# Decoding the first network's weights during the attention scores, with squares in PSUM and GpSimd clamping

## The chip, the core and the metric

The kernel runs on one core of a Trainium2 chip. The metric is the device time of one execution in microseconds (us), less is better. The engines go by the names of the profile: PE (TensorE matmul) with PEld (its weight loads), DVE (VectorE), ACT (ScalarE), POOL (GpSimd) and SP (SyncE, which here issues the DMAs). Each engine works through its own instructions in program order.

## The reference

An attention over channels is followed by two feed-forward networks, over 6016 tokens of 256 channels:

```python
qn = q / (np.linalg.norm(q, axis=1, keepdims=True) + 1e-06)
kn = k / (np.linalg.norm(k, axis=1, keepdims=True) + 1e-06)
s = kn.transpose(0, 2, 1) @ qn / tau            # 256 x 256
a = np.exp(s - s.max(-1, keepdims=True)); a /= a.sum(-1, keepdims=True) + 1e-09
x = v @ a                                       # 6016 x 256
h = x @ w_in1;  x = (h * np.cos(h)) @ w_out1    # 256 -> 2048 -> 256
h = x @ w_in2;  x = (h / (1 + np.exp(-h))) @ w_out2
```

q, k, v are float32, the four weight matrices float64 (4.19 MB each).

## The kernel before

It has three stages that bear on the change.

**Scores.** q and k lie together in 47 chunks of 128 rows, taken in 25 groups (`GROUPS`: two of one chunk, 22 of two, one of one). For each group g SP loads `qk` (eight buffers), PE multiplies into the scores S (`emit_scores`, L261), ACT squares into an SBUF tile `sq` with three buffers (L284), DVE adds to `acc` (L289). The scores of the last two groups (`LATE`) are emitted behind the norm matmuls N (L296, L300). Then come square roots, reciprocals, E (L320 to L325), the transposes to ET, eight warm-up matmuls among them.

**Weights.** A float64 matrix is loaded as 64-bit integers in pieces of 512 elements per partition and turned into float32 by `Weights.decode`: ACT takes the absolute value of the upper words (L136), GpSimd scales the lower words (L137), DVE clamps (L140), shifts (L141) and puts the sign in (L144), GpSimd adds the rounded low part (L147). For w_out1 GpSimd also makes a high and a low part (L150, L151): float32 products are done in three passes over high and low parts. Of the eight pieces of w_in1 two are loaded and decoded within the scores (`W1_LOADS`, `W1_DECODES`), the others between scores and fold; `to=w1` is a float32 tile.

**Fold and units.** The attention matrix is folded into w_in1: `emit_w(j)` multiplies ET by a quarter of w1 (pw, L356), ACT writes the high part of `wa[j]` (L362), DVE the low part (L364). Then 96 units follow (12 token blocks b of 512 or 496 tokens, eight units m each). A unit has `emit_h` (PE, twelve matmuls h, L395), `emit_first` (ACT L407, DVE L408), `emit_cos` (ACT L415, DVE L416), and, one unit later, `emit_split` (ACT L423 high, DVE L424 low) and, two units later, `emit_o1` (PE, twelve matmuls, L434). Units 2j and 2j + 1 of a block need `wa[j]` for h and `wo1[j]` for o1. The high and low parts of v for a block come from `load_v` and `split_v`. In block 0 each unit also loads and decodes a piece of w_out1; `emit_w(0)` to `emit_w(2)` stand ahead of unit 0, `emit_w(3)` ahead of unit 1, as does `load_v(1)`. From block 1 on the second network's weights are decoded in the same way, and the second network follows; that code is not touched.

PSUM has a pool `ps_o` (S, N, pw of j = 2 and 3, o1) and a pool `ps_h` (h, the transposes, pw of j = 0 and 1), two buffers each, allotted in turn.

Of the kernel before, what the change touches and what calls it, by code (L numbers as in the profile page):

```python
# [66 lines left out]
def attention_then_two_ffns(ctx: ExitStack, tc: tile.TileContext, qk, vT, tau, w_in1, w_out1, w_in2, w_out2, outT):  # L67
# [34 lines left out]
    class Weights:  # L102

        def __init__(self, name, srcs, parts=None, to=None, forms=None, pool=io, bufs=2):
            self.name, self.srcs, self.parts, self.to, self.pool, self.bufs = name, srcs, parts, to, pool, bufs
            self.forms = forms
            self.raws, self.loaded, self.decoded = {}, 0, 0

        def load(self, k=1):
            for i in range(self.loaded, min(self.loaded + k, len(self.srcs))):
                raw = self.pool.tile([P, PIECE], I64, tag="raw", name=f"raw_{self.name}{i}", bufs=self.bufs)
# [3 lines left out]
                self.loaded = i + 1  # L117

        def decode(self):
# [5 lines left out]
            a = self.srcs[i].shape[1]  # L125
            if self.to is None:
                t = io.tile([P, NS * P], F32, tag="wv", name=f"wv_{self.name}{i}")
                v = t[:, :PIECE].rearrange("p (a b) -> p a b", a=a)
            else:
                v = self.to[i]  # L130
            vi = v.bitcast(I32)

            def word(t, d):
                return raw.bitcast(d).rearrange("p (a b t) -> p a b t", a=a, t=2)[:, :, :, t]

            nc.scalar.activation(v, word(1, F32), AF.Abs)  # L136
# [4 lines left out]
            nc.vector.tensor_scalar(  # L141
                out=vi, in0=vi, scalar1=3, scalar2=0x3FFFFFFF, op0=ALU.logical_shift_left, op1=ALU.bitwise_and
            )
            nc.vector.scalar_tensor_tensor(  # L144
                out=vi, in0=word(1, I32), scalar=-0x40000000, in1=vi, op0=ALU.bitwise_and, op1=ALU.bitwise_or
            )
            nc.gpsimd.tensor_tensor(out=vi, in0=vi, in1=word(0, I32), op=ALU.add)  # L147
            if self.parts is not None:
                hi, lo = self.parts[i]
                nc.gpsimd.tensor_scalar(out=hi, in0=v, scalar1=1.0, scalar2=1.0, op0=ALU.mult, op1=ALU.mult)  # L150
                nc.gpsimd.tensor_tensor(out=lo, in0=v, in1=hi.bitcast(F32), op=ALU.subtract)  # L151
            if self.forms is not None:
                self.forms(i, t.rearrange("p (s b) -> p s b", b=P))

# [10 lines left out]

    def w_in(w, name, parts=None, to=None, **kw):
        n = PIECE // CH
        src = w.rearrange("(a p) f -> p a f", p=P)
        cut = [slice(j * n, (j + 1) * n) for j in range(NPIECE)]
        return Weights(  # L170
            name,
            [src[:, :, c] for c in cut],
            parts and [[t[:, :, c] for t in parts] for c in cut],
            None if to is None else [to[:, :, c] for c in cut],
            **kw,
        )

    def w_out(w, name, **kw):
        n = PIECE // C
# [639 lines left out]
```

## Time and profile before

| | |
|---|---|
| median of 3 runs | 1044.47 us (1042.96 to 1044.87) |
| the profiled execution | 1042.51 us, its span 1040.7 us |
| PE busy | 1010.5 us, 97% |
| DVE busy | 927.2 us, 89% |
| ACT busy | 751.7 us, 72% |
| POOL busy | 326.1 us, 31% |
| mean granted clock of TensorE | 0.995 |
| HBM traffic | 68.75 MB read, 39.65 MB written |

The page gives one execution as the profiler recorded it. In its slices of a fortieth of the span, PE shows 8 to 9 tenths in the first five and 9 in nearly all others. Busy shares are averages over stages with different limits, so the stages have to be looked at one by one: a view of windows gives each engine's busy time in a stretch, the granted clock (1.00 is 2.4 GHz, 0.50 is 1.2 GHz) and the DMA rate; the chain of waits goes back from the last instruction to what released each; the timeline lists instructions in order, with the idle time of the engine before each and what ended it; the view of a tile lists the instructions that read or write it.

### The profile page before, as it was taken

The page shows a single profiled execution, that of the slowest core. Times are in us where ns is not written, and L with a number is a line of the kernel's source. Part 1 is how long each engine was busy: PE and PEld are TensorE (multiplying, and loading weights), DVE is VectorE, ACT ScalarE, POOL GpSimd, SP SyncE. Part 2 cuts the span into 40 slices and gives each one's busy share as a digit, 9 for nine tenths or more (in the row PEclk, how much of TensorE's full clock was granted, in tenths as well). Part 3 has the DMA queues.
Part 4 walks back from the last instruction along what each step waited for, and adds up shares of the span by engine and source line. Part 5 has one row for each costly group of instructions (what it writes and reads, how often), then busy time and mean ns, then how long its engine had stood idle before and what let it go on. Part 6 is the DMA issues. An engine that isn't in the chain of part 4 may idle for free.

```text
span 1040.7 us, 17012 instructions
## 1 busy us (share of the span) xinstructions
PE 1010.5 (97%) x6593; PEld 936.3 (90%) x6593; DVE 927.2 (89%) x1166; ACT 751.7 (72%) x1194; POOL 326.1 (31%) x301
## 2 busy tenths in 40 slices
PE   8977899999999999999999799999999999999998
PEld 7846788888998988899998799999999999999998
DVE  6989999999999899988778689999989989899997
ACT  6545567667666766666666688888887887887885
POOL 2357754646655466450100011111111111111110
PEclk9989999999999999999999999999999999999999
DMA  9822212242351532532046650220220221122001
GB/s 354 288 69 87 81 41 91 77 164 103 116 187 30 170 124 76 179 124 72 17 161 242 250 227 12 83 90 11 80 90 22 69 89 55 45 80 88 13 11 40
DMA packets 56544, 109.49 MB, mean 105 GB/s; under 512 B 2832, under 2 KB 37648, under 8 KB 56464
## 3 DMA queue, kind: packets, MB, share of 16 engines
q1 hardware_dynamic: 56320, 108.28, 30.5%
q8 instruction: 52, 0.85, 0.3%
q14 instruction: 28, 0.23, 0.1%
q10 hardware_dynamic: 144, 0.13, 0.0%
HBM read 68.75 MB, written 39.65 MB: 104 GB/s over the span
## 4 chain that ended last, share of the span: by engine, by line
PE 83%; DVE 12%; ACT 2%; DMA 1%; issue 1%; SPq 0%; DVEq 0%; ACTq 0%
PE o L499 20%; PE h L395 20%; PE o L434 20%; PE xz L499 12%; PE ys L499 9%; DVE acc L289 2%; DVE lo L424 2%; DVE t L408 2%; DVE t L416 1%; PE pw L356 1%; DMA qk<-qk_dram 1%; DVE wv_wo L144 1%; DVE wv_wo L140 1%; DVE wv_wo L141 1%; ACT t L407 0%
## 5 line engine op out<-in xcount | busy, mean ns | idle before, releaser
L458 DVE TENSOR_TENSOR lo<-t,hi 128x744 fp32r<-128x744 f32 (+3 forms) x190 | 207.5, 1095 | 34.4 <-ACT hi L455 33.1
L499 PE MATMUL o<-hi,wo 128*128 128x248 f32 (+1 forms) x1330 | 232.6, 275 | 0.0
L450 POOL TENSOR_TENSOR t<-t 128x248 f32<-128x248 f32 (+1 forms) x94 | 67.8, 721 | 456.0 <-DVE t L449 407.8
L455 ACT ACTIVATE hi<-t 128x744 fp32r<-128x744 f32 (+3 forms) x190 | 178.5, 940 | 32.5 <-PE o L499 31.6
L499 PEld LDWEIGHTS o<-hi,wo 128*128 128x128 f32 x1330 | 201.8, 192 | 0.0
L395 PE MATMUL h<-xhi,wa 128*128 128x496 f32 (+1 forms) x768 | 195.9, 378 | 3.1 <-DVE wa L364 3.1
L434 PE MATMUL o<-hi,wo 128*128 128x496 f32 (+1 forms) x768 | 193.9, 375 | 0.0
L499 PE MATMUL o<-lo,wo 128*128 128x248 f32 (+1 forms) x665 | 182.9, 275 | 0.0
L415 ACT ACTIVATE t<-t,half_pi 128x992 f32<-128x992 f32 (+1 forms) x96 | 108.7, 1133 | 81.7 <-DVE t L408 81.6
L395 PEld LDWEIGHTS h<-xhi,wa 128*128 128x128 f32 x768 | 146.1, 190 | 22.0 <-issue 4.4
L434 PEld LDWEIGHTS o<-hi,wo 128*128 128x128 f32 x768 | 145.0, 189 | 17.1
L407 ACT ACTIVATE t<-h 128x992 int32<-128x992 f32 (+1 forms) x96 | 96.5, 1005 | 80.1 <-PE h L395 71.0
L408 DVE SCALAR_TENSOR_TENSOR t<-t,h 128x992 f32<-128x992 int32 (+1 forms) x96 | 114.8, 1196 | 41.5 <-ACT t L407 41.3
L499 PE MATMUL xz<-x2hi,wi 128*128 128x248 f32 (+1 forms) x768 | 143.7, 275 | 0.0
L424 DVE TENSOR_TENSOR lo<-t,hi 128x992 fp32r<-128x992 f32 (+1 forms) x96 | 141.6, 1474 | 1.2 <-ACT hi L423 1.2
L499 PEld LDWEIGHTS o<-lo,wo 128*128 128x128 f32 x665 | 127.7, 192 | 0.0
L434 PE MATMUL o<-lo,wo 128*128 128x496 f32 (+1 forms) x384 | 114.2, 379 | 9.9 <-DVE lo L424 9.9
L416 DVE TENSOR_TENSOR t<-h,t 128x992 f32<-128x992 f32 (+1 forms) x96 | 114.9, 1197 | 5.6 <-ACT t L415 1.2
L499 PEld LDWEIGHTS xz<-x2hi,wi 128*128 128x128 f32 x768 | 116.6, 192 | 0.1
L499 PE MATMUL ys<-x2hi,wi 128*128 128x248 f32 (+1 forms) x576 | 112.2, 276 | 3.9 <-ACT u L774 3.1
L395 PE MATMUL h<-xlo,wa 128*128 128x496 f32 (+1 forms) x384 | 113.3, 377 | 0.0
L499 PE MATMUL xz<-x2lo,wi 128*128 128x248 f32 (+1 forms) x384 | 105.6, 275 | 0.0
(128 smaller groups left out, 1679.4 us busy)
## 6 DMA issues: line engine op xcount, KB each, us to landing
qk<-qk_dram SPq DMA_DIRECT2D x22, 512.0 KB, 7.3
raw_wo<-w_out_dram SPq DMA_DIRECT2D x16, 512.0 KB, 5.0
xshi<-yhi SPq DMA_DIRECT2D x8, 868.0 KB, 5.9
xslo<-ylo SPq DMA_DIRECT2D x8, 868.0 KB, 6.9
x2hi<-xshi SPq DMA_DIRECT2D x8, 868.0 KB, 5.6
x2lo<-xslo SPq DMA_DIRECT2D x8, 868.0 KB, 7.7
wo_dram<-stage_wo SPq DMA_DIRECT2D x7, 896.0 KB, 4.5
wo<-wo_dram SPq DMA_DIRECT2D x7, 896.0 KB, 7.5
```

What stands on the lines that cost most here:

```text
L289: nc.vector.tensor_tensor(out=acc[:, :n], in0=acc[:, :n], in1=sq[:, :n], op=ALU.add)
L395: nc.tensor.matmul(hp[:, s, :n], lhsT, rhs, start=(i == 0), stop=(i == len(todo) - 1))
L407: nc.scalar.activation(k, hp[:, :, :n], AF.Copy, scale=1.0 / TWO_PI, bias=0.25)
L408: nc.vector.scalar_tensor_tensor(out=t[:, :, :n], in0=k, scalar=-TWO_PI, in1=hp[:, :, :n], op0=ALU.mult, op1=ALU.add)
L415: nc.scalar.activation(t[:, :, :n], t[:, :, :n], AF.Sin, bias=half_pi)
L416: nc.vector.tensor_tensor(out=t[:, :, :n], in0=hp[:, :, :n], in1=t[:, :, :n], op=ALU.mult)
L424: nc.vector.tensor_tensor(out=lo[:, :, :n], in0=t[:, :, :n], in1=hi[:, :, :n].bitcast(F32), op=ALU.subtract)
L434: nc.tensor.matmul(o[:, e, :n], wo1_at(i, f)[:, e * P : (e + 1) * P], columns(parts[k][:, s, :n]), start=(f == 0 and (i, k) == PASSES[0]), ...
L450: eng.tensor_tensor(out=t[:, 7, :c], in0=t[:, 3, :c], in1=t[:, 6, :c], op=ALU.subtract)
L455: nc.scalar.activation(hi[:, sl, :c], t[:, 1:][:, sl, :c], AF.Copy)
L458: nc.vector.tensor_tensor(out=lo[:, sl, :c], in0=t[:, 1:][:, sl, :c], in1=hi[:, sl, :c].bitcast(F32), op=ALU.subtract)
L499: nc.tensor.matmul(out, w[:, p, ka - 1], columns(x[r][:, kb - 1, : out.shape[-1]]), start=(start and i == 0), stop=(stop and i == 2), skip ...
```

## The change

- Pieces of w_in1 and w_out1 have 1024 elements (`LARGE`), four for each matrix, from a pool of three raw buffers that both share.
- `decode` is cut into `begin` (ACT absolute value, GpSimd scaling, and the clamp, now on GpSimd), `join` (DVE shift and sign, GpSimd add) and `split` (high part by a copy on ACT, low part on GpSimd). The second network's pieces go on in the old form.
- w_in1: loads at groups 0, 6, 12, 18, `begin` at 2, 8, 14, 20, `join` at 4, 10, 16, 22, all within the scores. v's first block is loaded at group 15 and split at group 21. Nothing is decoded between scores and fold.
- Squares go to a PSUM tile of `ps_h` (two buffers) instead of SBUF (three).
- The norms of q come ahead of those of k; ten warm-up matmuls instead of eight.
- `emit_w(0)` and `emit_w(1)` stand ahead of unit 0, `emit_w(2)` at unit 1, `emit_w(3)` at unit 3. w_out1's steps follow `WO1_STEPS`, one entry for each unit of block 0, with one `begin` and `join` ahead of `emit_w(0)` and one `begin` behind `emit_w(1)`.
- `pro.close()`, the pools behind it and `load_v(1)` move from unit 1 to unit 7; the second network's first two loads both stand at unit 7.

```diff
+W1_LOADS = range(0, 24, 6)
+W1_BEGIN = range(2, 26, 6)
+W1_JOIN = range(4, 28, 6)
+V_LOAD, V_SPLIT = 15, 21
+WO1_STEPS = [("split", "join"), ("load", "begin"), ("split",), ("join", "begin"), ("split",), ("join",), ("split",), ()]
...
+        def round_low(self, raw):
+            low = self.word(raw, 0, I32)
+            nc.gpsimd.tensor_scalar(
+                out=low, in0=low.bitcast(U32), scalar1=2.0**-29, scalar2=1.0, op0=ALU.mult, op1=ALU.mult
+            )
+        def shift_and_sign(self, raw, v):
+            vi = v.bitcast(I32)
+            nc.vector.tensor_scalar(
+                out=vi, in0=vi, scalar1=3, scalar2=0x3FFFFFFF, op0=ALU.logical_shift_left, op1=ALU.bitwise_and
+            )
+            nc.vector.scalar_tensor_tensor(
+                out=vi, in0=self.word(raw, 1, I32), scalar=-0x40000000, in1=vi, op0=ALU.bitwise_and, op1=ALU.bitwise_or
+            )
+            nc.gpsimd.tensor_tensor(out=vi, in0=vi, in1=self.word(raw, 0, I32), op=ALU.add)
...
+        def begin(self):
...
+            nc.scalar.activation(v, self.word(raw, 1, F32), AF.Abs)
+            self.round_low(raw)
+            nc.gpsimd.tensor_scalar(out=v, in0=v, scalar1=WORD_MIN, scalar2=WORD_MAX, op0=ALU.max, op1=ALU.min)
+            self.begun.append((i, raw, v))
+        def join(self):
+            i, raw, v = self.begun.pop(0)
+            self.shift_and_sign(raw, v)
+            self.joined.append((i, v))
+        def split(self):
+            i, v = self.joined.pop(0)
+            hi, lo = self.parts[i]
+            nc.scalar.activation(hi, v, AF.Copy)
+            nc.gpsimd.tensor_tensor(out=lo, in0=v, in1=hi.bitcast(F32), op=ALU.subtract)
...
         if g in W1_LOADS:
             W1.load()
-        sq = ep.tile([P, GMAX, 2 * C], F32, tag="sq", name=f"sq{g}", bufs=3)
+        if g == V_LOAD:
+            vraw0 = load_v(0, split=False)
+        sq = ps_h.tile([P, GMAX, 2 * C], F32, tag="h", name=f"sq{g}")
...
-        if g in W1_DECODES:
-            W1.decode()
+        if g in W1_BEGIN:
+            W1.begin()
+        if g in W1_JOIN:
+            W1.join()
+        if g == V_SPLIT:
+            split_v(0, vraw0, nc.scalar)
+    WO1.load(2)
...
-    while W1.loaded - W1.decoded < 4:
-        W1.load()
-    vraw0 = load_v(0, split=False)
-    for _ in range(2):
-        W1.decode()
-        W1.load()
...
-    for _ in range(3):
-        W1.decode()
-        W1.load()
-    split_v(0, vraw0, nc.scalar)
-    W1.decode()
-    WO1.load(2)
     early.close()
...
-            W1.decode()
-    for j in range(3):
-        emit_w(j)
+    WO1.begin()
+    WO1.join()
+    emit_w(0)
+    emit_w(1)
     WO1.load()
-    WO1.decode()
+    WO1.begin()
...
         if i == 1:
+            emit_w(2)
+        if i == 3:
             emit_w(3)
+        if i == NPAIR - 1:
             pro.close()
...
         if b == 0:
-            WO1.load()
-            WO1.decode()
-            if m >= NPAIR - 2:
-                WI2.load()
+            for step in WO1_STEPS[m]:
+                getattr(WO1, step)()
+            if m == NPAIR - 1:
+                WI2.load(2)
```

## Rows read from the trace of the kernel before

**Rows 1.** Windows: busy us (instructions) per engine, granted clock, DMA share, GB/s.
```profile
128.60:133.79 5.19, 5.19 (x26) 4.54 (x24) 4.52 (x5) 3.55 (x5) 0.93 (x1) 1.00 0.02 5
...
400.00:500.00 100.00, 100.00 (x479) 90.10 (x478) 88.13 (x82) 68.44 (x73) 45.74 (x34) 1.00 0.32 102
69.98:128.61 58.63, 49.93 (x201) 39.61 (x201) 55.57 (x54) 31.32 (x34) 43.15 (x35) 0.94 0.26 81
44.23:69.98 25.75, 19.63 (x74) 11.84 (x72) 23.37 (x34) 12.27 (x22) 13.83 (x12) 0.93 0.28 92
```

**Rows 2.** Chain of waits, 40 to 132 us: start, length, what.
```profile
43.54 0.69 DVE acc L289
...
47.61 1.02 DVE w L144
...
52.17 0.49 DVE E L320
```

**Rows 3.** Timeline of PE: start, length, line, tiles, count [idle before, releaser].
```profile
44.96 1.03 PE L296 MATMUL N<-acc,ones 128*128 128x256 f32 x4
...
46.63 2.84 PE L261 MATMUL S<-qk 128*128 128x256 f32 x12
49.31 1.95 PE L332 MATMUL pt<-ones 128*128 128x128 f32 x16
...
55.12 5.28 PE L356 MATMUL pw<-w,ET 128*128 128x512 f32 x9
...
55.12 11.72 PE L356 MATMUL pw<-w,ET 128*128 128x512 f32 x24
...
69.98 1.10 PE L395 MATMUL h<-xhi,wa 128*128 128x512 f32 x4 [3.14 <-DVE wa L364]
```

**Rows 4.** Scores: a window, the views of acc and sq (min/median/max ns), ACT's timeline.
```profile
20.00:30.00 10.00, 10.00 (x48) 8.81 (x47) 9.52 (x9) 7.23 (x8) 3.65 (x2) 1.00 1.03 408
...
L289 DVE TENSOR_TENSOR acc<-acc,sq x23: 692/1225/2133, 8.0 to 43.5; 128x1024 f32<-128x1024 f32 x22, 128x512 f32<-128x512 f32 x1
...
L284 ACT ACTIVATE sq<-qk x25: 630/1057/1062, 3.5 to 40.6; 128x1024 f32<-128x1024 f32 x22, 128x512 f32<-128x512 f32 x3
...
14.85 1.06 ACT L284 ACTIVATE sq<-qk 128x1024 f32<-128x1024 f32 x1 [1.57 <-DMA qk<-qk_dram]
```

**Rows 5.** Views of the tiles w (decode of w_in1) and xhi: min/median/max ns.
```profile
L136 ACT ACTIVATE w<-raw_w x8: 644/658/689, 19.7 to 58.7; 128x512 f32<-128x512 f32 x8
...
L141 DVE TENSOR_SCALAR w<-w x8: 427/907/1402, 21.5 to 64.3; 128x512 int32<-128x512 int32 x8
L144 DVE SCALAR_TENSOR_TENSOR w<-raw_w,w x8: 692/852/2773, 22.0 to 65.7; 128x512 int32<-128x512 int32 x8
...
L219 POOL TENSOR_TENSOR xlo<-vraw,xhi x3: 2471/2587/2832, 65.4 to 148.3; 128x1024 fp32r<-128x1024 f32 x3
L216 POOL TENSOR_SCALAR xhi<-vraw x2: 1609/2070/2532, 87.2 to 145.7; 128x1024 fp32r<-128x1024 f32 x2
L214 ACT ACTIVATE xhi<-vraw x1: 1157/1157/1157, 57.7 to 57.7; 128x1024 fp32r<-128x1024 f32 x1
```

**Rows 6.** The clock: one PE row, and windows of 1 us (PE busy, granted clock).
```profile
100.85 0.70 PE L434 MATMUL o<-lo,wo 128*128 128x512 f32 x2 [2.57 <-DVE lo L424]
...
72.00:73.00 1.00, 1.00 (x4) 0.50 0.00 0
...
102.00:103.00 1.00, 1.00 (x4) 0.50 0.67 258
```

**Rows 7.** Units 0 to 8: views of the tiles wv_wo, t and pw, min/median/max ns.
```profile
L147 POOL TENSOR_TENSOR wv_wo<-wv_wo,raw_wo x8: 1282/1300/1308, 74.1 to 124.3; 128x512 int32<-128x512 int32 x8
L150 POOL TENSOR_SCALAR wo<-wv_wo x8: 618/1472/1477, 75.5 to 125.7; 128x512 fp32r<-128x512 f32 x8
...
L416 DVE TENSOR_TENSOR t<-h,t x9: 1209/1211/1225, 77.7 to 130.6; 128x1024 f32<-128x1024 f32 x9
L424 DVE TENSOR_TENSOR lo<-t,hi x8: 1480/1568/2292, 82.9 to 129.0; 128x1024 fp32r<-128x1024 f32 x8
...
L364 DVE SCALAR_TENSOR_TENSOR wa<-pw,rs,wa x8: 734/735/768, 68.4 to 81.2; 128x512 fp32r<-128x512 f32 x8
```

More of the change, by code (lines that the diff above doesn't have):

```diff
@@ L51 @@
 LATE = 2
-W1_LOADS = (6, 10)
-W1_DECODES = (10, 15)
+WARM = 10
+W1_LOADS = range(0, 24, 6)
[3 more added lines that the diff above has]
+WO1_STEPS = [("split", "join"), ("load", "begin"), ("split",), ("join", "begin"), ("split",), ("join",), ("split",), ()]
 assert sum(GROUPS) == NCK
@@ L59 @@
 PIECE = 512
-NPIECE = C * DFF // P // PIECE
+LARGE = 1024
 WORD_MIN = 2.0 ** (0x380 // 8 - 127)
@@ L102, in attention_then_two_ffns, with __init__ @@
     class Weights:
-        def __init__(self, name, srcs, parts=None, to=None, forms=None, pool=io, bufs=2):
+        def __init__(self, name, srcs, parts=None, to=None, forms=None, pool=io, bufs=2, size=PIECE):
             self.name, self.srcs, self.parts, self.to, self.pool, self.bufs = name, srcs, parts, to, pool, bufs
-            self.forms = forms
+            self.forms, self.size = forms, size
             self.raws, self.loaded, self.decoded = {}, 0, 0
+            self.begun, self.joined = [], []
         def load(self, k=1):
             for i in range(self.loaded, min(self.loaded + k, len(self.srcs))):
-                raw = self.pool.tile([P, PIECE], I64, tag="raw", name=f"raw_{self.name}{i}", bufs=self.bufs)
+                raw = self.pool.tile([P, self.size], I64, tag="raw", name=f"raw_{self.name}{i}", bufs=self.bufs)
                 src = self.srcs[i]
@@ L117, in load, with view, word @@
                 self.loaded = i + 1
+        def view(self, i):
+            a = self.srcs[i].shape[1]
+            if self.to is not None:
+                return None, self.to[i]
+            t = io.tile([P, NS * P], F32, tag="wv", name=f"wv_{self.name}{i}")
+            return t, t[:, : self.size].rearrange("p (a b) -> p a b", a=a)
+        def word(self, raw, t, d):
+            a = self.srcs[0].shape[1]
+            return raw.bitcast(d).rearrange("p (a b t) -> p a b t", a=a, t=2)[:, :, :, t]
+        def round_low(self, raw):
[12 more added lines that the diff above has]
+            nc.gpsimd.tensor_tensor(out=vi, in0=vi, in1=self.word(raw, 0, I32), op=ALU.add)
         def decode(self):
@@ L124, in decode @@
             raw = self.raws.pop(i)
[L125 to L136, printed above, removed]
@@ L137, in decode @@
-            nc.gpsimd.tensor_scalar(
-                out=word(0, I32), in0=word(0, U32), scalar1=2.0**-29, scalar2=1.0, op0=ALU.mult, op1=ALU.mult
-            )
-            nc.vector.tensor_scalar(out=v, in0=v, scalar1=WORD_MIN, scalar2=WORD_MAX, op0=ALU.max, op1=ALU.min)
[L141 to L153, printed above, removed]
+            t, v = self.view(i)
@@ new lines, in decode @@
+            nc.scalar.activation(v, self.word(raw, 1, F32), AF.Abs)
+            self.round_low(raw)
+            nc.vector.tensor_scalar(out=v, in0=v, scalar1=WORD_MIN, scalar2=WORD_MAX, op0=ALU.max, op1=ALU.min)
+            self.shift_and_sign(raw, v)
+            self.forms(i, t.rearrange("p (s b) -> p s b", b=P))
+        def begin(self):
+            i = self.decoded
+            self.decoded += 1
+            raw = self.raws.pop(i)
+            _, v = self.view(i)
+            nc.scalar.activation(v, self.word(raw, 1, F32), AF.Abs)
+            self.round_low(raw)
+            nc.gpsimd.tensor_scalar(out=v, in0=v, scalar1=WORD_MIN, scalar2=WORD_MAX, op0=ALU.max, op1=ALU.min)
+            self.begun.append((i, raw, v))
@@ L164, in weight_forms, with w_in, w_out @@
             nc.gpsimd.tensor_tensor(out=lo, in0=t[:, 0], in1=hi.bitcast(F32), op=ALU.subtract)
-    def w_in(w, name, parts=None, to=None, **kw):
-        n = PIECE // CH
+    def w_in(w, name, to=None, size=PIECE, **kw):
+        n = size // CH
         src = w.rearrange("(a p) f -> p a f", p=P)
[L169 to L179, printed above, removed]
+        cut = [slice(j * n, (j + 1) * n) for j in range(DFF // n)]
+        to = None if to is None else [to[:, :, c] for c in cut]
+        return Weights(name, [src[:, :, c] for c in cut], to=to, size=size, **kw)
+    def w_out(w, name, size=PIECE, **kw):
+        n = size // C
         src = w.rearrange("(f p) e -> p f e", p=P)
-        return Weights(name, [src[:, n * j : n * (j + 1), :] for j in range(NPIECE)], **kw)
+        return Weights(name, [src[:, n * j : n * (j + 1), :] for j in range(NF // n)], size=size, **kw)
     def columns(t):
@@ L247, in attention_then_two_ffns @@
     rs = pp.tile([P, CH], F32, name="rs")
-    W1 = w_in(w_in1, "w1", to=w1, pool=pp, bufs=4)
+    W1 = w_in(w_in1, "w1", to=w1, pool=pp, bufs=3, size=LARGE)
     WO1 = w_out(
@@ L251, in attention_then_two_ffns @@
         "wo1",
-        parts=[[wo1[j // 2][:, i, j % 2].rearrange("p (f e) -> p f e", e=C) for i in range(2)] for j in range(NPIECE)],
+        parts=[[t[:, i].rearrange("p m (f e) -> p (m f) e", e=C) for i in range(2)] for t in wo1],
+        pool=pp,
+        bufs=3,
+        size=LARGE,
     )
@@ L302, in attention_then_two_ffns @@
         emit_scores(g)
-    while W1.loaded - W1.decoded < 4:
-        W1.load()
-    vraw0 = load_v(0, split=False)
-    for _ in range(2):
-        W1.decode()
-        W1.load()
+    nc.scalar.activation(rq, N[:, 0, :C], AF.Sqrt)
     nc.scalar.activation(rk, N[:, 1, :CH], AF.Sqrt)
-    nc.scalar.activation(rq, N[:, 0, :C], AF.Sqrt)
     nc.scalar.activation(warm, eps, AF.Exp)
+    nc.vector.tensor_scalar_add(rq, rq, 1e-6)
+    nc.vector.reciprocal(rq, rq)
     nc.vector.tensor_scalar_add(rk, rk, 1e-6)
@@ L329, in attention_then_two_ffns @@
         if a == 0:
-            for _ in range(8):
+            for _ in range(WARM):
                 nc.tensor.matmul(pt[:, 1, :P], ones, ones, start=True, stop=True)
```

3 lines of the change are left out of this document (1 added, 2 removed).

## Prediction

> **What bounds the kernel now.** I read the page's busy shares first, then the busy time by stage, then the chain of waits where a stage is not full. PE and DVE are both busy for most of the span, a mean over unlike stages. By stage [rows 1] PE has no idle time from 128.6 us on: a unit of the first network takes 5.18 us there, two times 2.59 us of matmuls, and a later stretch looks the same. So PE sets the pace of the last 912 us, the change leaves that work alone, and what is won or lost before 128.6 us arrives at the end one for one. From 44.23 to 69.98 us PE is busy for 19.63 of 25.75 us, and from 69.98 to 128.61 us for 49.93 of 58.63 us at a mean granted clock of 0.94; DVE has 23.37 and 55.57 us there. That is the room. The chain of waits names the owners [rows 2]: DVE adding squares to 44.23 us, DVE decoding weights to 48.6 us, DVE normalising to 52.2 us; then PE folds, waits for DVE's low parts of wa until 69.98 us [rows 3], and from there DVE again.
>
> Five marks carry the sum: the norm matmuls N start at 44.96 us, E at 52.17, the fold pw at 55.12, unit 0's first matmul (h0) at 69.98 [rows 2, 3], unit 9's (h9) at 128.61.
>
> **Step 1, the scores, +8.2 us.** All 4.19 MB of w_in1 and the 0.52 MB of v now stand in the queue ahead of the last qk group; before, 1.05 MB did. The queue gives 408 GB/s, so 0.524 MB (a group of two chunks) takes 1.29 us. Group 7 is squared at 14.85 us, as it lands, behind 4.19 MB or 10.3 us of transfer: the stream counts as if begun at 4.5 us [rows 4]. After the change the last group comes behind 12.32 + 4.19 + 0.52 = 17.04 MB, 41.8 us: it lands at 46.3 us, group 19 at 40.5, with 1.29 us from group to group between. DVE ended its sum at 44.23 us until now, so the queue alone costs about 3.4 us (sq 0.63 and acc 0.69 us behind the landing [rows 4]).
> The order on ACT and DVE costs more. ACT from group 19, 1.06 us a square [rows 4]: sq19 to 41.6, sq20 to 42.9, the Abs of the fourth piece, sq21, the v copy (1.16 us [rows 5]), sq22 to 47.2. The Abs of 1024 elements is not in the trace: it lies between a square of that size (1.06) and two Abs of 512 (2 x 0.66 [rows 5]); I take 1.1, since size and not operation sets these rows. On DVE acc22 runs to 48.45, and join() of the fourth piece stands next, ahead of acc23 and acc24. Its two operations take 0.43 and 0.69 us at 512 elements when undisturbed [rows 5]; at 1024 I take 0.7 and 1.22, less than double because the start is paid once. Bounds: 1.1 (as for 512), and 4.5 if the first waits out GpSimd's xlo, 2.5 to 2.8 us [rows 5]. So join to 50.4, acc23 to 51.7, acc24 to 52.5, and N 0.7 us behind, as before: 53.2 against 44.96. The floor is 48.3 us (last landing, square, add, 0.7).
> Squares in PSUM: the add takes 1.22 us in the median and up to 2.13 us [rows 4]; DVE's product that reads h from PSUM stays at 1.21 to 1.23 us while GpSimd works [rows 7]. I take 1.25 for all adds; the stretched ones go, but lie under the queue now. The Trainium skill (Perfetto Trace Analysis, Optimizing Scalar/DVE Operations) gives DVE a start of about 60 ns on SBUF and 125 ns on PSUM; by that estimate the 22 adds would cost 1.4 us more, 0.3 us of it in this tail. The rows speak against it: 1.21 with PSUM, 1.22 without.
>
> **Step 2, N to E, -1.2 us.** The two decodes between acc and the normalising leave DVE's path [rows 2]. DVE would then be ready for E some 3.2 us after N, where 5.4 us stood. But now PE's late scores come last: N 1.7 us to their start, 2.8 us for them [rows 3]. And PE has been idle. Its earlier scores run up to N at 44.96 now, and to about 47.6 when one load (2.6 us) precedes group 1; to 53.2 that is 5.6 us. After idles of 2.57 us and 3.14 us the granted clock fell to 0.5, that is to 1.2 GHz [rows 3, 6], for about 3.3 us each time. Such a stretch costs 1.65 us of work; I charge 1.4 (0 to 1.7). E at 53.2 + 1.8 + 2.8 + 1.4 = 59.2: 6.0 us where 7.2 stood.
>
> **Step 3, E to pw, +0.5 us.** 2.95 us before. The warm-ups, now ten (eight took 1.95 us [rows 3]), run behind the late scores and hold the first transpose some 0.5 us. pw at 62.65.
>
> **Step 4, pw to h0, -8.0 us.** Before 14.86: 24 records in 11.72 us, nine of them in 5.28 us at the low clock, then 3.14 us of wait for wa [rows 3]. Now two folds, 16 records at 0.43 us ((11.72 - 5.28) / 15), 6.9 us, the clock being up because PE has worked since 53.2. Covered by the second fold is the low part of wa[0], which stands on DVE behind WO1's first join, which waits for GpSimd's clamp: Abs after the last exp and the table load to about 64.2, clamp 1.1 (between 0.62 for 512 and 1.61 for the strided copy of 1024 [rows 5, 7]), join to 67.3, two low parts of 0.74 us [rows 7] to 68.8. h0 is due at 69.5; the cover is 0.7 us, and if clamp and join are stretched as in the rows up to 1.5 us are lost. h0 at 69.5 against 69.98: steps 1 to 4 cancel.
>
> **Step 5, h0 to h9, -4.4 us.** Before 58.63. PE's own work: nine h and seven o1 of 2.59 us (41.4) and now two folds (6.9): 48.3 us. DVE's unit is 1.21 + 1.49 + 1.21 us [rows 7], nine are 35.2; the clamps and half the starts are gone; three joins at 2.8 us (1.9 undisturbed, 3.5 at twice the medians' sum [rows 5]) and four low parts of wa (2.9) remain: 46.5, under PE's 48.3. So the bound moves from DVE to PE. ACT gains three Abs, four copies and two more scaled copies, some 9 us beside 28 us of units: free. GpSimd has three each of round, clamp and add, four subtractions, near 1.1 and 2.5 us (1.30 at 512, 2.59 at 1024 [rows 5, 7]), 24 us with v's 4.5: it fits. Three waits come on top. (a) o1(0) needs the low part of unit 0, which DVE reaches behind join 1 and wa[2]: 2.0 us (1.4 to 3.4). (b) load_v(1) moves from unit 1 to unit 7. Its DMA may go early, since SP is not held, but its split on GpSimd stands behind the last weight subtraction, which waits for ACT's copy behind unit 6's sine: 1.06 + 2.5 + 1.6 + 2.5 = 7.7 us after that sine. The sine ends some 3.5 us after h6; PE comes to h8 7.8 us after h6 (o1, h7, o1) and wants xlo 0.9 us later. 11.2 against 8.7: a wait of 2.5 us (0 to 4.3). (c) L424 beside GpSimd, up to 2.29 us [rows 7]: 1.5 us. 48.3 + 2.0 + 2.5 + 1.5 = 54.3; h9 at 123.8. Later, o1 of block 1 takes the buffer of block 0's o1, since the third fold is allotted between them: up to 0.3 us, within the rounding.
>
> **Sum.** +8.2 - 1.2 + 0.5 - 8.0 - 4.4 = -4.9 us. The profiled execution took 1042.51 us (span 1040.7): 1037.6. The median of the three runs, 1044.47, lies 1.96 us higher, and the forecast of a median is 1039.6.
>
> **Rivals.**
> A. The tail of the scores is not late: ACT and DVE keep up, N starts near 48.3, no low clock follows. 4.9 + 1.4 us more are won: -11.2, a median of 1033.3. For it: between squares ACT mostly waited for the queue. Against: Abs, the v copy and the join stand in the tail in program order.
> B. Slower: GpSimd takes the SBUF port from DVE in units 0 to 7. Its operations on 1024 elements are twice as long, so a blocked DVE operation waits up to 2.5 us. If the eight L424 take 2.29 instead of 1.49 (+6.4, 1.5 charged) and each of three joins waits out one add (+7.2), 12.1 us are added, less the wait (b) of 2.5 that lies under it: 1037.6 + 9.6 profiled, a median of 1049.2. It decides from about 7 us of extra delay on. For it: joins' operations reached 1.40 and 2.77 us [rows 5]. Against: the median L424 is 1.57. The Trainium skill (Perfetto Trace Analysis, the same section) says that moving work between these two engines may not help, as one locks the port they share; the add of 2.13 us agrees.
> C. No net change: the tail costs 2.5 us more (join blocked by xlo), wa[0] 1.5 us, or units stay at DVE's pace for half of B: 1042.5 to 1046.5.
> That the change does not do what it says is unlikely: the order is the program's.
>
> **Chances.** Forecast (2 to 9 us won) 0.54; A 0.17; C 0.14; B 0.15. Under 0.2% (2.1 us) counts as no difference, about what this measurement can tell. Faster 0.71, same 0.14, slower 0.15. The range takes in A and C: 1032 to 1046.5; the likeliest case alone is 1035.5 to 1042.4.
>
> **What would show it.** N near 53 us behind the fourth join (A: near 48); half clock in N and the late scores; no idle time of PE between the second fold and h0; after the first o1 PE idle under 0.5 us a unit (B: 1 to 2 us in every unit); unit 8's h waiting some 2 us for GpSimd's xlo. The forecast is wrong above all if the queue keeps another pace with 1 MB loads, or if the tail of ACT and DVE runs in another rhythm.

## The result, and the profile after

The changed kernel takes 1053.66 us in the median (1053.12 to 1053.66, 4 runs) beside 1043.72 us (1041.92 to 1044.87, 4 runs) of the kernel before in the same comparison: a ratio of 1.0096, 95% interval 1.0078 to 1.0113. It is 9.94 us slower; the forecast was 1039.6 us, faster. The profiled execution's span is 1051.9 us (before 1040.7), the mean granted clock 0.989 (before 0.995).

The windows of the changed kernel, in the columns of [rows 1]: the scores up to N, from N to E, from unit 0's first matmul to unit 9's, and one unit behind it.

```profile
3.59:55.36 51.77, 41.62 (x176) 35.28 (x176) 38.01 (x34) 28.96 (x30) 30.48 (x13) 0.96 0.93 364
55.36:63.23 7.87, 7.87 (x26) 6.75 (x27) 2.46 (x6) 1.93 (x4) 1.65 (x2) 0.58 0.41 134
75.34:139.48 64.14, 55.79 (x208) 43.20 (x209) 46.04 (x37) 35.66 (x37) 39.28 (x17) 0.89 0.12 41
139.48:144.66 5.18, 5.18 (x25) 4.54 (x24) 3.47 (x4) 3.00 (x4) 0.00 (x0) 1.00 0.01 3
```

From h9 on a unit still takes 5.18 us, and what follows h9 takes 912.4 us, 912.1 before. So the loss is made before h9, as every gain would have been; the forecast had the place right and the sum wrong. The timeline of PE, as in [rows 3]:

```profile
9.77 39.55 PE L288 MATMUL S<-qk 128*128 128x256 f32 x172 [4.11 <-DMA qk<-qk_dram]
55.36 2.07 PE L329 MATMUL N<-acc,ones 128*128 128x256 f32 x4 [6.04 <-DVE acc L318]
58.80 4.39 PE L288 MATMUL S<-qk 128*128 128x256 f32 x12
66.25 7.10 PE L377 MATMUL pw<-w,ET 128*128 128x512 f32 x16
75.34 1.78 PE L417 MATMUL h<-xhi,wa 128*128 128x512 f32 x4 [1.99 <-DVE wa L385]
92.54 1.12 PE L456 MATMUL o<-lo,wo 128*128 128x512 f32 x2 [3.21 <-DVE lo L446]
120.41 0.70 PE L456 MATMUL o<-hi,wo 128*128 128x512 f32 x2 [2.20 <-POOL wo L183]
130.66 2.07 PE L417 MATMUL h<-xhi,wa 128*128 128x512 f32 x4 [2.53 <-POOL xhi L240]
133.16 1.22 PE L417 MATMUL h<-xlo,wa 128*128 128x512 f32 x2 [0.42 <-POOL xlo L243]
```

The five marks, in us:

| mark | before | forecast | after | after − forecast |
|---|---|---|---|---|
| N | 44.96 | 53.2 | 55.36 | +2.2 |
| E | 52.17 | 59.2 | 63.23 | +4.0 |
| pw | 55.12 | 62.65 | 66.25 | +3.6 |
| h0 | 69.98 | 69.5 | 75.34 | +5.8 |
| h9 | 128.61 | 123.8 | 139.48 | +15.7 |

More than half of the miss, 9.8 us, arises between h0 and h9. The operations of GpSimd and DVE there, as in [rows 5, 7] (count: min/median/max ns; L171 is the clamp, L143 the shift, L149 GpSimd's add, L446 the low part of a unit), and last the add of the squares in the scores:

```profile
L171 POOL TENSOR_SCALAR wv_wo<-wv_wo x4: 3622/3622/3623, 68.3 to 114.4; 128x1024 f32<-128x1024 f32 x4
L143 DVE TENSOR_SCALAR wv_wo<-wv_wo x4: 684/1738/2830, 71.9 to 118.1; 128x1024 int32<-128x1024 int32 x4
L149 POOL TENSOR_TENSOR wv_wo<-wv_wo,raw_wo x4: 2387/2409/2416, 74.0 to 122.6; 128x1024 int32<-128x1024 int32 x4
L446 DVE TENSOR_TENSOR lo<-t,hi x8: 1218/1254/2600, 91.2 to 139.2; 128x1024 fp32r<-128x1024 f32 x8
L318 DVE TENSOR_TENSOR acc<-acc,sq x23: 689/1221/1225, 12.2 to 54.6; 128x1024 f32<-128x1024 f32 x22, 128x512 f32<-128x512 f32 x1
```

The clamp takes 3.62 us, every time, where the forecast had 1.1. ACT's timeline shows group 19's square, and the timeline of DVE what stands behind it and behind the clamp: join's shift in the tail of the scores, and the one ahead of `emit_w(0)`.

```profile
42.13 1.03 ACT L313 ACTIVATE sq<-qk 128x1024 f32<-128x1024 f32 x1 [2.81 <-DMA qk<-qk_dram]
```
```profile
48.44 1.22 DVE L318 TENSOR_TENSOR acc<-acc,sq 128x1024 f32<-128x1024 f32 x1 [0.77 <-ACT sq L313]
49.58 2.55 DVE L143 TENSOR_SCALAR w<-w 128x1024 int32<-128x1024 int32 x1
...
71.92 0.69 DVE L143 TENSOR_SCALAR wv_wo<-wv_wo 128x1024 int32<-128x1024 int32 x1 [5.04 <-POOL wv_wo L171]
```

### The profile page after: what moved, and what is told of

The parts are those of the page before. It is cut to its first block, busy times and chain, and to the rows that moved or that the text cites. A ratio compares the mean times of both kernels' runs of the same rounds, so it can differ in the third digit from the quotient of the medians.

```text
span 1051.9 us, 16908 instructions
## 1 busy us (share of the span) xinstructions
PE 1015.6 (97%) x6597; PEld 940.5 (89%) x6597; DVE 906.6 (86%) x1134; ACT 753.7 (72%) x1190; POOL 334.8 (32%) x281
## 4 chain that ended last, share of the span: by engine, by line
PE 85%; DVE 6%; ACT 3%; DMA 2%; POOL 2%; issue 1%; SPq 0%; DVEq 0%; ACTq 0%; POOLq 0%
PE h L417 21%; PE o L456 20%; PE o L521 20%; PE xz L521 12%; PE ys L521 9%; PE S L288 3%; DMA qk<-qk_dram 2%; DVE t L430 1%; DVE lo L446 1%; PE pw L377 1%; DVE wv_wo L143 1%; ACT t L429 1%; DVE y L472 0%; POOL wv_wo L149 0%; DVE t L438 0%
## 5 line engine op out<-in xcount | busy, mean ns | idle before, releaser
L446 DVE TENSOR_TENSOR lo<-t,hi 128x992 fp32r<-128x992 f32 (+1 forms) x96 | 141.6, 1475 | 1.2 <-ACT hi L445 1.2
```

The source lines that it names most:

```text
L446: nc.vector.tensor_tensor(out=lo[:, :, :n], in0=t[:, :, :n], in1=hi[:, :, :n].bitcast(F32), op=ALU.subtract)
```

## The experiments

Each run is given by its excess over the kernel before in its own comparison; the changed kernel's is +9.94 us. Theory 1 is that the clamp's length on GpSimd, and what waits for it in program order, makes the loss; the rivals are the tail of the scores, the place of `load_v(1)`, and contention between GpSimd and DVE. Where an expectation names 9.1 or 9.8 us as a difference of runs, it compares their times without the kernel before of each comparison; the text goes by the excesses. Marks such as N and h0 are of one profiled execution of each run.

**The clamp back on DVE.**

```diff
 def begin(self):
-    nc.gpsimd.tensor_scalar(out=v, in0=v, scalar1=WORD_MIN, scalar2=WORD_MAX, op0=ALU.max, op1=ALU.min)
 def join(self):
+    nc.vector.tensor_scalar(out=v, in0=v, scalar1=WORD_MIN, scalar2=WORD_MAX, op0=ALU.max, op1=ALU.min)
```

> The changed kernel with the clamp back on DVE (at the head of join), all else kept. Theory 1 (the clamp is the dear part: each max/min on GpSimd takes 3.62 us for 1024 elements where the same engine's multiplication takes 1.1 us): the clamp takes 0.69 us on DVE; N comes 1 to 1.5 us earlier than 55.36, the 1.99 us wait for wa ahead of h0 and the 2.2 us wait of o1(4) for wo go, the wait ahead of h8 shrinks: 5 to 8 us less than the changed kernel's 1053.66. Theory 2 (any further work on GpSimd holds the port, whichever operation it is; the clamp is a small part of it): at most 2.5 us less.

Measured 1051.40 us, ratio 1.0074 (1.0055 to 1.0093), +8.15. The wait for wa is gone, but the first o1 waits 3.87 us for DVE instead of 3.21. Only 1.8 us are won, well under what theory 1 expected, and within the intervals of the two runs. In the profiled execution h9 comes 2.8 us earlier and 1.4 of it go again behind h9. PE still waits for a low part twice (3.87 us and a new 1.94); that DVE, which now has the clamp's 0.69 us ahead of every shift, pays for what GpSimd no longer does is the likely reason, argued and not shown by a run.

**A short instruction in the clamp's place.** GpSimd multiplies by 1.0 (the clamp is left out), so that place and waits stay and only the length changes.

```diff
-nc.gpsimd.tensor_scalar(out=v, in0=v, scalar1=WORD_MIN, scalar2=WORD_MAX, op0=ALU.max, op1=ALU.min)
+nc.gpsimd.tensor_scalar(out=v, in0=v, scalar1=1.0, scalar2=1.0, op0=ALU.mult, op1=ALU.mult)
```

> The changed kernel with the clamp left out of the first network's weights: GpSimd does a multiplication by 1.0 twice in its place, same tile, same size, same waits. Theory 1 (max and min are slow on GpSimd, not the extra instruction): the instruction falls from 3.62 to about 1.1 us and the time by 4 to 7 us. Theory 2 (an extra GpSimd instruction costs by its place in the queue and the port): it stays near 3.6 us because it waits out DVE's operations, or falls with less than 2.5 us for the whole.

Measured 1048.18 us, ratio 1.0048 (1.0033 to 1.0063), +4.93. The view of wv_wo in this run:

```profile
L171 POOL TENSOR_SCALAR wv_wo<-wv_wo x4: 1043/1044/1053, 67.6 to 109.9; 128x1024 f32<-128x1024 f32 x4
L143 DVE TENSOR_SCALAR wv_wo<-wv_wo x4: 683/1210/2778, 68.7 to 113.1; 128x1024 int32<-128x1024 int32 x4
```

The forecast's 1.1 us was the time of a multiplication of this size, and the same instruction with max and min takes 3.5 times as long (3.622 / 1.044). That alone is worth 5.0 us, half of the loss (2.6 to 7.4 by the intervals of the two runs). The shift still takes up to 2.78 us: that stretch does not come from the clamp.

**`load_v(1)` at unit 3 instead of unit 7.**

```diff
         if i == 3:
             emit_w(3)
+            load_v(1)
...
-            load_v(1)
         hp = emit_h(u)
```

> The changed kernel with the load and split of v's second block put at unit 3 instead of unit 7, where GpSimd is idle for 9 us. Theory 1 (unit 8's h waits for that split and then runs at the low clock): h8 starts with no wait of PE on xhi or xlo, and unit 9's first matmul, at 139.48 us, comes 4.5 to 6.5 us earlier; the time falls as much. Theory 2 (PE waits there for other work as well, so that another wait takes its place): less than 2 us.

Measured 1048.14 us, ratio 1.0050 (1.0035 to 1.0065), +4.89. From h0 to h9:

```profile
78.44:134.47 56.03, 50.68 (x208) 40.36 (x209) 45.88 (x37) 35.84 (x37) 40.58 (x17) 0.97 0.13 47
```

PE's work falls from 55.79 to 50.68 us, its idle time from 8.35 to 5.35, at a clock of 0.97 instead of 0.89. From h7 to h8 it is 5.30 us instead of 7.99, from h8 to h9 5.18 instead of 8.82. So a wait of 2.95 us (2.53 + 0.42) cost 6.3: PE works on at 1.2 GHz behind it. Nearly all of the other 1.8 us by which the stretch is shorter do not come from the edit: from h0 to h1 it is 5.69 us instead of 7.38, since the granted clock stays at 1.00 behind the wait of 1.76 us ahead of h0, where it fell behind 1.99 us in the changed kernel. Nor does the edit move N, which comes at 57.38 here and at 55.36 there with the same code up to unit 3: marks of single executions are sure to some 2 us.

**The tail of the scores freed**: the fourth `begin` and v's split behind the loop, the fourth `join` behind the softmax.

```diff
+W1_BEGIN = range(2, 20, 6)
+W1_JOIN = range(4, 22, 6)
...
     WO1.load(2)
+    W1.begin()
+    split_v(0, vraw0, nc.scalar)
...
     nc.vector.reciprocal(rs, rs)
+    W1.join()
```

> The changed kernel with the fourth piece's absolute value and clamp and v's split put behind the last square, and its join put behind the softmax, so that nothing stands between the last squares and additions. The loads stay where they are. Theory 1 (half of the lateness of the scores is the order on ACT and DVE, and the clock that falls meanwhile): N starts at 50 to 51 us instead of 55.36, N and the late scores take 4.7 us instead of 7.9, the time falls by 5 to 8 us. Theory 2 (the queue with 4.7 MB ahead of the last group sets it): N moves by less than 2 us.

Measured 1052.40 us, ratio 1.0093 (1.0078 to 1.0108), +9.15. PE's timeline, then DVE's:

```profile
51.34 1.13 PE L329 MATMUL N<-acc,ones 128*128 128x256 f32 x4 [1.18 <-DVE acc L318]
74.07 2.05 PE L418 MATMUL h<-xhi,wa 128*128 128x512 f32 x4 [6.26 <-DVE wa L386]
```
```profile
70.65 0.69 DVE L143 TENSOR_SCALAR wv_wo<-wv_wo 128x1024 int32<-128x1024 int32 x1 [7.47 <-POOL wv_wo L171]
```

The steps the forecast named for the tail are real: without them N starts 4.0 us earlier, its four matmuls at full clock (1.13 us, 2.07 in the changed kernel; the granted clock is 0.50 only from 53.5 to 56.5 us), and pw at 60.70, 5.5 earlier. But h0 comes only 1.3 us earlier: WO1's clamp, pushed behind the fourth piece's add on GpSimd, ends only 1.3 us earlier, and PE waits 6.26 us for what follows it.

**Squares in SBUF again**, all else as changed.

```diff
-        sq = ps_h.tile([P, GMAX, 2 * C], F32, tag="h", name=f"sq{g}")
+        sq = ep.tile([P, GMAX, 2 * C], F32, tag="sq", name=f"sq{g}", bufs=3)
```

> The changed kernel with the squares back in SBUF (three buffers), all else kept. Theory 1 (in PSUM the squares keep DVE's additions off the port that GpSimd holds): additions beside the 3.62 us clamp are stretched to as much as 3.6 us, N starts 1 to 4 us after 55.36, the time rises by 1 to 4 us. Theory 2 (the queue hides it): N and the time within 1 us of the changed kernel.

Measured 1063.41 us, ratio 1.0201 (1.0186 to 1.0216), +20.92. The views of acc and w, and PE's timeline:

```profile
L318 DVE TENSOR_TENSOR acc<-acc,sq x23: 1218/1226/3246, 12.6 to 61.9; 128x1024 f32<-128x1024 f32 x22, 128x512 f32<-128x512 f32 x1
L149 POOL TENSOR_TENSOR w<-w,raw_w x4: 3221/3249/3253, 19.4 to 60.8; 128x1024 int32<-128x1024 int32 x4
L171 POOL TENSOR_SCALAR w<-w x4: 3622/4446/4467, 13.7 to 51.0; 128x1024 f32<-128x1024 f32 x4
```
```profile
64.61 2.08 PE L329 MATMUL N<-acc,ones 128*128 128x256 f32 x4 [14.86 <-DVE acc L318]
```

N comes 9.25 us later, far more than was expected: both sides are stretched, DVE's add to 3.25 us, GpSimd's add from 2.40 to 3.25 and its clamp from 3.62 to 4.45. Without the squares in PSUM, decoding during the scores in this order costs 11 us more.

**Three edits at once**: the clamp on DVE, the freed tail, `load_v(1)` at unit 3 (the edits above).

> The changed kernel with the clamp on DVE, v's second block at unit 3, and nothing between the last squares and additions, all three at once. Theory 1 (three separate costs; alone the freed tail gained 4.0 us at N and lost them in front of h0, where GpSimd's clamp of w_out1's first piece now came last): N near 51, h0 at 67.5 to 68.5 with under 0.5 us of wait, no wait at h8, 1040 to 1042.5 us in all. Theory 2 (each fix uncovers the next wait): no more than the sum of the single gains, 9.1 us, so 1044.5 us or more.

Measured 1045.55 us, ratio 1.0027 (1.0018 to 1.0037), +3.06: 6.9 us of the changed kernel's 9.94 are won, where the single runs add up to 7.6. The timeline of DVE shows what is left:

```profile
62.32 0.69 DVE L175 TENSOR_SCALAR wv_wo<-wv_wo 128x1024 f32<-128x1024 f32 x1
63.05 2.78 DVE L143 TENSOR_SCALAR wv_wo<-wv_wo 128x1024 int32<-128x1024 int32 x1
65.86 1.99 DVE L146 SCALAR_TENSOR_TENSOR wv_wo<-raw_wo,wv_wo 128x1024 int32<-128x1024 int32 x1
67.77 2.71 DVE L386 SCALAR_TENSOR_TENSOR wa<-pw,rs,wa 128x512 fp32r<-128x512 f32 x4
```

Two joins in a row on DVE, the second stretched while GpSimd adds for the first, stand ahead of the low parts of wa; h0 waits 3.30 us.

**Loads later**, on top of this: w_in1's pieces at groups 4, 9 and 14, the fourth and v behind the last q and k; the fourth `begin` and v's split go behind the square roots.

```diff
+W1_LOADS = (4, 9, 14)
+W1_BEGIN = (7, 12, 17)
+W1_JOIN = (8, 13, 18)
...
+    W1.load()
+    vraw0 = load_v(0, split=False)
     WO1.load(2)
```

> As e6, and the loads of w_in1 at groups 4, 9 and 14, each decoded four groups later, the fourth piece and v loaded behind the last qk group, the fourth piece decoded and v split behind the square roots. Theory 1 (what is left of the lateness of the scores is the queue: 3.4 us at its end and one load ahead of group 1): PE works from its second group on as before, N starts at 45.5 to 47.5 us, and the time is 3.5 to 5 us under e6. Theory 2 (DVE, with three joins among its additions, sets the end of the scores): N at 49 us or later, less than 2 us under e6.

Measured 1044.71 us, ratio 1.0025 (1.0010 to 1.0041), +2.22. N starts at 49.30 instead of 50.61, but waits 2.67 us for DVE's add: with the queue relieved DVE's joins set the end of the scores. h0 comes no earlier (70.42, 69.31 before this edit).

**The fourth fold as filling**: `emit_w(3)` ahead of the first o1, and w_out1's second `join` one unit later.

```diff
+WO1_STEPS = [("split",), ("join", "load", "begin"), ("split",), ("join", "begin"), ("split",), ("join",), ("split",), ()]
...
         if i == 3:
-            emit_w(3)
             load_v(1)
...
             v = units[i - LAG]
+            if i == LAG:
+                emit_w(3)
             emit_o1(v, parts.pop(i - LAG))
```

> As e7, and the fourth fold put ahead of the first o1 instead of ahead of unit 3's h, and w_out1's second join one unit later. Theory 1 (PE's wait of 3.2 us at the first o1 comes from the join that stands on DVE ahead of unit 0's low part): the wait falls under 0.5 us and the time by 2.5 to 4 us against e7. Theory 2 (the wait only moves to the next unit): less than 1 us.

Measured 1043.24 us, ratio 1.0002 (0.9990 to 1.0015), +0.75. The first o1 no longer waits; a new wait of 3.93 us stands at the fourth. Which half of the edit gains and which gives back was not run apart.

**Joins where DVE has nothing due**: w_in1's third behind the last add, WO1's first and w_in1's fourth behind the second fold.

```diff
+W1_JOIN = (8, 13)
...
+    W1.join()
     W1.load()
...
     WO1.begin()
-    WO1.join()
     emit_w(0)
     emit_w(1)
+    WO1.join()
+    W1.join()
```

> As e8, with DVE's joins put where DVE was idle: the third join of w_in1 behind the last addition (DVE waits there for the norms), w_out1's first and w_in1's fourth join behind the second fold instead of ahead of the first. Theory 1 (what kept e6 to e8 level with the kernel before is the place of the joins on DVE, ahead of N and of wa): N at 47 to 47.6 us, h0 at 61.5 to 63.5 with no wait for wa, unit 9 at 118 to 121.5, 1033 to 1037 us. Theory 2 (DVE and GpSimd are full in units 0 to 8 by the amount of decoding, wherever it starts): unit 9 at 124 or later and 1040 us or more.

Measured 1040.28 us, ratio 0.9979 (0.9969 to 0.9988), −2.63: faster than the kernel before. N starts at 46.84, h0 at 62.65 without a wait, both as theory 1 had it or earlier; but the time is that of theory 2 (1040 us or more), and h9, at 123.73, lies between the two. The next wait is on PE, and on DVE it is the same sight as before, ahead of unit 0's gate:

```profile
76.88 2.04 PE L419 MATMUL h<-xhi,wa 128*128 128x512 f32 x4 [5.12 <-DVE t L440]
```
```profile
66.52 0.69 DVE L143 TENSOR_SCALAR wv_wo<-wv_wo 128x1024 int32<-128x1024 int32 x1
67.25 1.22 DVE L146 SCALAR_TENSOR_TENSOR wv_wo<-raw_wo,wv_wo 128x1024 int32<-128x1024 int32 x1
68.39 0.69 DVE L175 TENSOR_SCALAR w<-w 128x1024 f32<-128x1024 f32 x1
69.12 2.78 DVE L143 TENSOR_SCALAR w<-w 128x1024 int32<-128x1024 int32 x1
```

**The kernel before with squares in PSUM**, and nothing else.

```diff
-        sq = ep.tile([P, GMAX, 2 * C], F32, tag="sq", name=f"sq{g}", bufs=3)
+        sq = ps_h.tile([P, GMAX, 2 * C], F32, tag="h", name=f"sq{g}")
```

> The kernel before with one part of the change alone: the squares in PSUM (two buffers). Theory 1 (this part pays only against much GpSimd work in the scores, as the 9.8 us of e5 show; here GpSimd has two pieces of 512 there, and PE's scores end at 45.1 us anyway): within 1.5 us of the kernel before. Theory 2 (it pays by itself): 3 us or more faster.

Measured 1041.20 us, ratio 0.9985 (0.9977 to 0.9994), −1.71. The longest add falls from 2133 ns [rows 4] to 1223, N comes 1.0 us earlier in the profiled execution, less than marks scatter. By itself the part is worth 1.7 us, beside four decodes in the scores 11: these two cases fit a saving that grows with GpSimd's work beside it.

**One join each side of the folds**: as two runs ago, but WO1's first join back ahead of the first fold, where DVE had nothing for 4.03 us.

```diff
     WO1.begin()
+    WO1.join()
     emit_w(0)
     emit_w(1)
-    WO1.join()
     W1.join()
```

> Edit on the run with the joins in the gaps (1040.28): the first join of the first output weights goes ahead of the first input fold of unit 0, into the 4 us in which VectorE has nothing queued at 57 to 61 us; only the input weights' fourth join stays behind the second fold, so that one join and not two stands ahead of unit 0's first gate on VectorE. Theory (what is lost after pw is VectorE's in-order queue): the wait of 5.12 us of the third h for t falls below 1.5 us, no wait for wa comes in its place, the span falls by 2 to 4 us and the time is 1036 to 1038.5 us. Rival (the join is stretched by GpSimd's work, or the wait moves to wa at the first h): a wait of 2 us or more for wa at the first h, and 1040 us or more.

Measured 1034.87 us (1034.27 to 1035.85), ratio 0.9935 (0.9923 to 0.9948), −7.26, better than its own theory had it. The timeline of PE:

```profile
72.34 1.10 PE L419 MATMUL h<-xhi,wa 128*128 128x512 f32 x4 [0.44 <-DVE t L440]
99.42 1.22 PE L458 MATMUL o<-lo,wo 128*128 128x512 f32 x2 [4.18 <-DVE lo L448]
```

The wait of 5.12 us is 0.44. What remains is one wait of 4.18 us for a low part, behind a join whose shift GpSimd's split of v stretches to 2.79 us. With the clamp on DVE and the steps of the change in this order the kernel beats both, the one before and the changed one. The decoding is the same as in the run of the joins in the gaps, and 4.6 us are won by its place alone.

Behind h9 913.8 us follow here, 912.1 in the kernel before. The 1.6 us between lie where PE turns to the second network. PE waits 2.18 us there in both; the same matmuls from there on take 3.58 us before, at a granted clock of 1.00, and 5.21 us here, where it is down to 0.52. The kernel before, then this run:

```profile
573.88 0.50 PE L699 MATMUL ys<-wo 128*128 128x256 f32 x2 [2.18 <-DVE t L416]
576.21 1.00 PE L434 MATMUL o<-hi,wo 128*128 128x496 f32 x4
```
```profile
564.78 0.50 PE L727 MATMUL ys<-wo 128*128 128x256 f32 x2 [2.18 <-DVE t L440]
567.82 1.86 PE L458 MATMUL o<-hi,wo 128*128 128x496 f32 x4
```

So the same wait costs its idle time in one execution and 1.6 us more in another.

**The kernel before with the clamp on GpSimd**, and nothing else.

```diff
+            eng = nc.vector if self.forms is not None else nc.gpsimd
-            nc.vector.tensor_scalar(out=v, in0=v, scalar1=WORD_MIN, scalar2=WORD_MAX, op0=ALU.max, op1=ALU.min)
+            eng.tensor_scalar(out=v, in0=v, scalar1=WORD_MIN, scalar2=WORD_MAX, op0=ALU.max, op1=ALU.min)
```

> The kernel before with one edit: the clamp of the weights' pieces (512 elements) is done on GpSimd and not on VectorE; squares, order of loads and folds stay. Theory 1 (the clamp on GpSimd is long, 3.62 us for 1024, so some 1.81 us for 512, and the rest of a join stands behind it in VectorE's queue): slower by 3 to 10 us, lost as waits of h and o for wa, wo or t between the first h and the end of the loads. Theory 2 (moving the clamp relieves VectorE, by some 0.4 us for each piece): 3 to 7 us faster, with the waits for VectorE shorter.

Measured 1073.21 us, ratio 1.0303 (1.0287 to 1.0318), +31.1: the sign of theory 1, three times its size. The view of wv_wo with its idle time, PE's timeline and DVE's:

```profile
L141 POOL TENSOR_SCALAR wv_wo<-wv_wo x8: 1913/1914/1916, 84.4 to 149.9; 128x512 f32<-128x512 f32 x8
...
  POOL wv_wo L141: 27.6, 8
```
```profile
83.65 2.04 PE L396 MATMUL h<-xhi,wa 128*128 128x512 f32 x4 [7.63 <-DVE wa L365]
113.17 1.22 PE L435 MATMUL o<-lo,wo 128*128 128x512 f32 x2 [5.33 <-DVE lo L425]
130.05 0.70 PE L435 MATMUL o<-lo,wo 128*128 128x512 f32 x2 [3.10 <-DVE lo L425]
138.59 0.95 PE L435 MATMUL o<-lo,wo 128*128 128x512 f32 x2 [3.10 <-DVE lo L425]
```
```profile
109.44 0.43 DVE L142 TENSOR_SCALAR wv_wo<-wv_wo 128x512 int32<-128x512 int32 x1 [7.66 <-POOL wv_wo L141]
```

The clamp takes 1.91 us for 512 elements, near the 1.81 that was taken as half of 3.62. What was missed is the queue: `decode` puts the clamp between ACT's and DVE's steps of one piece, so DVE stands still for it 27.6 us over w_out1's eight pieces, and everything behind it in DVE's order, the units' gates and low parts, stands too. It also stands 23.8 us for seven of w_in1's pieces: h0 comes 13.7 us later than in the kernel before, and h9 30.2. Where the clamp itself waits for GpSimd's split of v, one such wait is 7.66 us. In the changed kernel the clamp's length costs 5 us; that the cut into `begin` and `join` is what keeps it to that is likely, but no run has the changed kernel without the cut.

## Why the prediction was wrong, point by point

- **The steps that failed**: two terms. The clamp of a piece on GpSimd was sized at 1.1 us (step 4, and within "near 1.1" in step 5) and takes 3.62; that is worth 5.0 us of time. And step 5 counted PE's waits as idle time alone and put the half clock behind them at nothing; PE's work took 7.5 us more than its sum, nearly all of it the low clock, though the forecast's own rows showed 1.2 GHz behind waits of 2.57 and 3.14 us and step 2 charged for it. The rest of the miss is in steps 1 and 2, some 2 us each.
- **What bounds the kernel** was right: what follows h9 is untouched (912.0 to 914.5 us in all runs), and each microsecond ahead of it counts once. The room was where the forecast saw it; of the first five slices of PE's busy time two show 7 tenths, so they are 7 to 9 and not 8 to 9.
- **Step 1, N at 53.2: 55.36.** Right in kind: the tail of ACT and DVE, not the queue alone, ends the scores, and rival A did not happen. Group 19 lands at 42.1 us and not at 40.5. The pace was right (410 GB/s from 10 us on); but w_in1's first load stands near the head of the queue, PE waits 4.11 us for the next q and k, and the first 10 us move 2.2 MB where they moved 2.7 before, which is 1.1 us. The rest was not followed. That leaves acc22 1.1 us late. The fourth join's shift takes 2.55 us instead of 0.7, beside GpSimd's split of v; that adds 1.8, and N follows the last add 0.7 us sooner than was taken. The bound of 4.5 us for this join had it; the value chosen did not. The squares in PSUM were sized rightly: 1.25 us for every add was taken, and 1.225 is the longest. What the forecast did not say is how much hangs on them: without them the changed kernel takes 11 us more, with N 9.25 us later.
- **Step 2, 6.0 us from N to E: 7.87.** The half clock was foreseen, but not that it holds through the whole stretch (0.58 in the window): from N to the late scores it is 3.44 us where 1.8 was taken, and the scores take 4.39, near the 2.8 + 1.4 that stood for them and the clock together.
- **Step 3** held: 3.02 us, forecast 3.45.
- **Step 4, 6.85 us from pw to h0: 9.09.** Here the clamp's price tells first. The clamp of 1024 elements was sized at 1.1 us, between 0.62 and 1.61, from GpSimd's multiplications [rows 5, 7]; it is 3.62 us, outside the bounds. The rows of before show no max or min on GpSimd, and a bound from another operation of the same engine and size was no bound. DVE's join waits 5.04 us for it and h0 1.99, as the forecast had said for a cover that is gone.
- **Step 5, 54.3 us from h0 to h9: 64.14**, the largest miss. PE's work was 48.3 us by the sum and is 55.79; of the 7.5 us nearly all are the low clock (0.89 in the mean), for which the sum had nothing. The granted clock is 0.50 behind the waits of 1.99 us ahead of h0, of 3.21 and of 2.95 us, and stays at 1.00 behind the one of 2.20. The waits were 6.0 and are 8.4: (a) the first o1 3.21 instead of 2.0; (b) h8 2.95 instead of 2.5, from the right owner; w_out1's third piece 2.20, which the sum did not have and which the long clamp makes (in the run with the multiplication it is 0.61); (c) L424's 1.5 did not come. The sum counted three waits as their idle time only. The run with `load_v(1)` at unit 3 shows their price: 2.95 us of wait cost 6.3, the rest at 1.2 GHz behind it.
- **Rival B** had the sign and 1049.2 us, but not the mechanism that decided. Its main term, L424 at 2.29 us in every unit, is refuted: L446 has a median of 1254 ns, less than before (1568), though its longest is 2600, and from h0 to h9 PE waits for it once, the 3.21 us of (a). Its second term is there: shifts blocked up to 2.83 us. Slower was given 0.15.
- **Rival C**, no net change, had two of the blows that fell ahead of h0: a join blocked by v's split (1.85 us) and a late wa[0] (PE waits 1.99 us). It too had no price for the clock in units 0 to 8.
- **What made it slower**: by the marks, the change loses 10.4 us to N and 5.5 from h0 to h9, and wins 5.8 from pw to h0. Of this the clamp's length is 5.0 us and `load_v(1)` at unit 7 5.05 us, both shown by a run each; the tail of the scores is 4.0 us at N, but under 1 us of time by itself. These overlap, and there is the order of loads, joins and folds, worth 10.3 us between the run with three edits (+3.06) and the last of that line (−7.26), which keeps PSUM squares, large pieces and the first pieces' decodes within the scores. What each of these moves is worth alone was not run apart.
- **Open**: why the granted clock falls behind some waits of about 2 us and not behind others. Whether the wait of 4.18 us that is left can be taken away by moving v's split was not tried.

## What to carry to other kernels

A price is of an operation, not of an engine and a size: an operation that the trace does not show on an engine has no upper bound there, and where one stands in the middle of a chain ACT, GpSimd, DVE, its length is paid by all that DVE has queued behind. A wait of PE costs its idle time and, where the clock falls, the half clock behind it: 2.95 us of wait cost 6.3 here, while behind 2.20 us the clock did not fall. And before a step is moved, look for the stretch in which the engine it goes to has nothing due: the same join was free in a gap of 4 us, and seven microseconds later it was half of a wait of 5.12 us.

## What the runs showed of the hardware

- GpSimd's TENSOR_SCALAR with max and min on 128x1024 f32 takes 3.622 us, with two multiplications by 1.0 1.044 us; DVE does the clamp in 0.69 us. The Trainium skill (GPSIMD Engine Reference, 4.1 Engine selection) says that elementwise work with one input runs on GpSimd at roughly line rate. The multiplication bears that out, at 1.5 times DVE's time; the clamp, at 5.2 times, does not.
- DVE's add beside GpSimd takes up to 3.246 us with both inputs in SBUF and never over 1.225 us with one in PSUM; GpSimd's add and clamp are stretched too, from 2.40 to 3.25 us and from 3.62 to 4.45. The Trainium skill (SBUF — State Buffer, Who interferes with whom) says that DVE contends with GpSimd's reads where it takes two inputs from SBUF; its Summary: rules for kernel authors says that the one that comes second waits until the first has finished. These rows agree. So do the long shifts: the one of 2.55 us in the changed kernel and the one of 2.79 us in the fastest run each end 0.55 us behind GpSimd's split of v, and the one of 2.78 us ahead of unit 0's gate ends 0.57 us behind GpSimd's add.
- The start on PSUM that the forecast weighed (the Trainium skill, Perfetto Trace Analysis, Optimizing Scalar/DVE Operations) is not seen: 1.221 us in the median with PSUM, 1.226 without.
- TensorE's granted clock behind waits of PE: in the changed kernel it fell to 0.50 behind 1.99, 3.21 and 2.95 us and stayed at 1.00 behind 2.20; with `load_v(1)` at unit 3 it stayed at 1.00 behind 1.76 and 2.11. Behind the wait of 2.18 us at the turn to the second network it stayed in the kernel before and fell in the fastest run.
